# Linear attention into a routed mixture of experts: all row tiles of attention turned by VectorE, the first one-hot lanes by ScalarE, gates and routing half a pair of steps sooner

## The chip, the cores and the metric

The kernel runs on one core of a Trainium2 chip. The metric is the device time of one execution in microseconds; lower is better. TensorE (PE in the profile; PEld is its weight load) multiplies, VectorE (DVE) and ScalarE (ACT) work on tiles, GpSimd (POOL) multiplies by powers and issues the indirect transfers, SyncE (SP) issues nearly all other transfers. Each engine works through its own instructions in program order and waits at the head of its queue.

## The reference

Four sequences of 768 tokens, 8 heads of 64. Attention in blocks of 64: `intra = (q k^T * Dmask) v`, `inter = (q * lam^(pos+1)) kv_state`, then `kv_state = lam^64 * kv_state + (k * rev_pow)^T v`. The output, a row x of 512 numbers for each token, goes into a layer of 8 experts:

```python
logits = x @ w_gate                       # 8 numbers for each token
local_gate = sigmoid(x @ w_local)
e = argmax(logits) if s == 0 or local_gate < 0.5 else prev_e   # along the sequence
p = softmax(logits)
out[b, s] = p[e] * (relu(x[b, s] @ w1[e]) @ w2[e])
```

A token thus either takes its own best expert or that of its predecessor, and each row goes through one expert only.

## The kernel before

**Attention.** The tokens lie in 24 row tiles of 128 (`ORDER`: six chunks c of each of the four sequences b, so tile s is chunk s // 4 of sequence s % 4). A step s has five parts on TensorE: `scores` (into one of two pairs of PSUM banks, `sides`), `from_state` (queries times the state `kvs[b]`, into banks `po0`, `po1` for even s and `pl`, `pr` for odd s), `mix` (masked scores times values into the same banks; ScalarE copies the result to `xc[:, :, b]`), and `update` (keys times values, into the banks that held scores; VectorE adds the result to the state). VectorE's `masked` turns scores into `sm`, GpSimd's `prepare` makes the keys and queries with powers. From step 6 on two steps form a pair: the loop `for s in range(PAIRS, NS, 2)` issues the scores of s + 1 and s + 2, both `masked`, `from_state` of s and s + 1, what `middles[s]` lists, `mix` of both, what `betweens[s]` lists, `turn(s)`, `update` of both, the loads, what `lasts[s]` lists, `turn(s + 1)`. The order is written out by hand in a manual schedule for all five engines, so what stands earlier in this list is ahead in the engine's queue. Step s + 3's scores go into the same pair of banks as those of step s + 2 (s even).

**Rows.** `xc` holds x with features on partitions. The rows themselves go to `x_dram`, from which tiles of tokens of one expert are gathered later. There are two ways: `turned_rows` has VectorE transpose 32 x 32 blocks of a tile into a group of four tiles (`TURNED` says at which step), and `group_out` writes the group in four transfers whose pieces are 512 bytes; `rows_of` has TensorE turn the tile in four matmuls, ScalarE copy it, and SyncE write it in pieces of 2 KB. Tiles 0 to 13 and 20 to 22 take the first way, 14 to 19 and 23 the second. Each loop step sends up to two waiting group transfers; the rest follow the loop, ahead of the weights of the second tile of experts.

**Routing.** `gates(k)` multiplies chunk k by the gate weights (ScalarE copies the product), `logits(k)` turns it back, VectorE reduces it into `lt`. Routing is done in three `PARTS` (tiles 0 to 7, 8 to 11, 12 to 23): `fresh_experts` marks each token's own expert, `along_sequences` carries the expert along the sequence (a test against zero, `stay`, and a scan), `experts_of` makes `hot`, `ranks` numbers the tokens of each expert (`place`), `masks` makes one-hot lanes from the place, `first_tiles` and `first_ends` choose the experts of the first KA = 3 tiles, `tokens_to_first_tiles`, `brought` and `by_slots` turn this into indices `gidx`, with which `ahead` gathers the first tiles from the rows of the first 12 tiles of attention.

**Experts.** After the loop come three full tiles (`hidden`, `output`, with the rest of the routing between) and then eight units, one for each expert, of sums and products of halves. The weights are 2 MB each (`w1t`, `w2t`, two buffers of each), loaded by SyncE.

Of the kernel before, what the change touches and what calls it, by code (L numbers as in the profile page):

```python
# [42 lines left out]
TURNED = {**{r: r + 1 if r < PAIRS else r // 2 * 2 + 2 for r in range(3 * B)}, 12: 15, 13: 16, 20: 22, 21: 22, 22: 23}  # L43
# [26 lines left out]
def kernel(  # L70
# [96 lines left out]
    kvs = []  # L167
    for b in range(B):
        kvs.append(pows.tile([P, A, DH], F32, name=f"kv{b}"))
# [74 lines left out]
    def from_state(s):  # L244
        b, c = ORDER[s]
        head = heads[s] = place_of(s)
        if c:
            kv, qd = kvs[b], qds.pop(s)
            for a in range(A):
                for u in range(2):  # L250
                    rows = slice(DH * u, DH * u + DH)
                    nc.tensor.matmul(head(a, u), lhsT=kv[rows, a], rhs=qd[rows, a],  # L252
                                     start=(a < 2), stop=False, skip_group_check=True)
# [16 lines left out]
    def update(s):  # L270
        b, c = ORDER[s]
        x = inp.pop(s)
        if c + 1 < NC:
            kv, vn = kvs[b], x[:, 2].rearrange("p (a u d) -> p a u d", u=2, d=DH)
# [14 lines left out]
    def rows_of(s, px=None):  # L289
        if px is None:  # L290
            px = pg.tile([P, DM], F32, name="pk1")
        for a in range(A):
            nc.tensor.transpose(px[:, P * a:P * a + P], xc[:, a, ORDER[s][0]], ident)
        if s + 1 < NS:
            xn = att.tile([P, DM], F32, name="xn", bufs=4)
        else:
            xn = xlast
        nc.scalar.copy(xn.rearrange("p (j d c) -> p j d c", j=4, c=QP), px.rearrange("p (d j c) -> p j d c", j=4, c=QP))


        nc.sync.dma_start(out=x_dram[P * s:P * s + P, :], in_=xn)

    groups = {}

    def turned_rows(s):

        k = s // B
        if k not in groups:
            if k + 1 == NC:
# [50 lines left out]
    def constants_1():  # L360
# [8 lines left out]
        nc.gpsimd.memset(onesb, 1.0)  # L369
        nc.gpsimd.memset(ones8, 1.0)  # L370
# [35 lines left out]
    place = route.tile([P, 2, NT], I32, name="place")  # L406
    late = route.tile([P, NA], F32, name="late")
    taken = route.tile([P, E], F32, name="taken")
# [32 lines left out]
    def along_sequences(i, pr=pr):  # L441
# [8 lines left out]
        nc.vector.tensor_scalar(stay, prow, 0.0, None, ALU.is_equal)  # L450
# [7 lines left out]
    def experts_of(i):  # L458
# [9 lines left out]
    def ranks(i, pr=pr):  # L468
# [23 lines left out]
        nc.vector.tensor_scalar(place[:, 0, lo:hi], rank, P - 1, None, ALU.bitwise_and)  # L492
        nc.vector.tensor_scalar(place[:, 1, lo:hi], rank, -P, None, ALU.bitwise_and)

    def masks(i):

        lo, hi = PARTS[i]
        lane = onehots[i] = (act if i == 2 else route).tile([P, hi - lo, P], BF16, name=f"lane{i}", bufs=1)
        nc.vector.tensor_tensor(lane, countb.unsqueeze(1).broadcast_to([P, hi - lo, P]),
# [47 lines left out]
    def first_tiles():  # L547

        tiles = multiples(0, NA, counts[1], ALU.is_ge, 1)
        table = nows["table"] = rt.tile([P, 2, E], F32, name="table0", bufs=1)  # L550
# [7 lines left out]
    def first_ends():  # L558

        table, ends, more, tiles = (nows[n] for n in ("table", "ends", "over", "tiles"))  # L560
# [7 lines left out]
        nc.vector.tensor_tensor(table[:, 0], ends, taken, ALU.subtract)  # L568
        nc.vector.tensor_copy(table[:, 1], taken)

    def tokens_to_first_tiles():
# [5 lines left out]
        nc.vector.scalar_tensor_tensor(to, late, float(P * AWAY), to, ALU.mult, ALU.add)  # L577
        owners(0, 0, KA, nows["ends"], 0)
# [966 lines left out]
```

## Time and profile before

| | |
|---|---|
| median of 3 runs | 403.49 us (403.45 to 404.9) |
| the profiled execution | 403.04 us, span 401.3 us, mean granted clock 0.997 |
| busy, share of the span | PE 97%, PEld 90%, DVE 74%, ACT 54%, POOL 46% |
| DMA | 90.67 MB, mean 226 GB/s |

The span reaches from the first to the last instruction. Attention fills the first 90 us; the first hidden layer of an expert starts at 90.91 us, the units at 137.62 us. A matmul's end in the profile is modelled, since matmuls overlap in the array; the distance between the starts of two groups is the better measure of what a group costs. An engine's idle time is given with the instruction that ended it.

### The profile page before, as it was taken

How to read it: one execution, taken by the hardware profiler on the slowest of the kernel's cores; microseconds unless marked ns; L12 is line 12 of the kernel's file. 1: busy time of each engine (PE TensorE's matmuls, PEld its weight loads, DVE VectorE, ACT ScalarE, POOL GpSimd, SP SyncE). 2: the span in 40 equal slices, each digit the busy share in tenths (PEclk: the TensorE clock that was granted, in tenths of full speed). 3: DMA queues.
4: the chain of work that ended last, by engine and by line, in shares of the span. 5: the costliest groups of instructions: out<-in, count | busy, mean ns of one | idle time of the engine just before them, and what ended most of it. 6: DMA issues, size and time to landing. Idle time of an engine off the chain costs nothing. (4 is left out here: it accounts for less than half of the span.)

```text
span 401.3 us, 9727 instructions
## 1 busy us (share of the span) xinstructions
PE 391.1 (97%) x3729; PEld 362.8 (90%) x3729; DVE 297.7 (74%) x570; ACT 215.4 (54%) x658; POOL 184.4 (46%) x228
## 2 busy tenths in 40 slices
PE   7999999999999999999999999999999999999994
PEld 6788988878679699999999999999999999999983
DVE  6876989947845889878868768686776868677931
ACT  4236355446715758767557755944854684460310
POOL 5589677330125312174272277157227605701741
PEclk9999999999999999999999999999999999999998
DMA  7999999999999977357346266273545606100101
GB/s 272 417 425 402 416 399 389 340 311 284 390 399 372 406 274 263 96 185 279 118 171 222 70 233 223 97 235 94 206 119 200 265 29 237 51 0 8 45 35 60
DMA packets 37145, 90.67 MB, mean 226 GB/s; under 512 B 3344, under 2 KB 12064, under 8 KB 35424
## 3 DMA queue, kind: packets, MB, share of 16 engines
q1 hardware_dynamic: 31920, 76.57, 52.1%
q0 software_dynamic: 5152, 13.38, 9.5%
q8 instruction: 31, 0.51, 0.5%
q14 instruction: 26, 0.21, 0.2%
q10 hardware_dynamic: 16, 0.00, 0.0%
HBM read 81.55 MB, written 12.91 MB: 235 GB/s over the span
## 5 line engine op out<-in xcount | busy, mean ns | idle before, releaser
L1207 POOL DMA_INDIRECT out_dram<-yq,sidxq x80 | 89.2, 1115 | 103.3 <-DVE yq L1195 69.9
L1152 PE MATMUL ps<-arena,s 128*128 128x148 f32 (+7 forms) x384 | 63.1, 307 | 0.0
L1152 PEld LDWEIGHTS ps<-arena,s 128*128 128x128 f32 x384 | 57.3, 190 | 0.4 <-DVE part L1336 0.3
L807 POOL DMA_INDIRECT xg<-x_dram,gidx x27 | 30.1, 1117 | 52.5 <-DVE w L1123 14.6
L1152 PE MATMUL po<-arena,w 128*128 128x148 f32 (+7 forms) x256 | 41.9, 307 | 0.0
L1152 PE MATMUL ps<-arena,w 128*128 128x148 f32 (+7 forms) x256 | 41.9, 307 | 0.0
L828 ACT COPY arena<-xlast 32x128 f32<-32x128 f32 x128 | 37.8, 295 | 4.8 <-DVE xlast L821 2.1
L1152 PEld LDWEIGHTS ps<-arena,w 128*128 128x128 f32 x256 | 38.3, 190 | 0.5 <-issue 0.5
L1152 PEld LDWEIGHTS po<-arena,w 128*128 128x128 f32 x256 | 38.2, 190 | 0.0
L188 POOL TENSOR_TENSOR qd<-inp,lamq 128x256 f32<-128x256 f32 x40 | 29.5, 759 | 16.7 <-DMA inp<-in_qkv_dram 6.5
L828 ACT COPY arena<-lg 32x128 f32<-32x128 f32 x120 | 35.5, 296 | 2.6
L1190 PE MATMUL pk<-h,w 128*128 128x148 f32 (+6 forms) x224 | 35.1, 310 | 0.0
L1190 PE MATMUL pk<-hsum,s 128*128 128x148 f32 (+6 forms) x224 | 35.1, 310 | 0.0
L1190 PEld LDWEIGHTS pk<-h,w 128*128 128x128 f32 x224 | 33.4, 190 | 0.0
L1190 PEld LDWEIGHTS pk<-hsum,s 128*128 128x128 f32 x224 | 33.4, 190 | 0.0
L256 ACT ACTIVATE kv<-kv,lamq 128x64 f32<-128x64 f32 x64 | 16.4, 335 | 24.0 <-PE po L252 24.0
L1171 ACT COPY arena<-xlast 32x128 f32<-32x128 f32 x88 | 26.9, 305 | 1.9
L194 POOL TENSOR_TENSOR kd<-inp,rev 128x256 f32<-128x256 f32 x40 | 23.8, 615 | 7.9 <-DMA inp<-in_qkv_dram 7.8
L1308 ACT ACTIVATE h<-ps 128x296 f32<-128x296 f32 (+6 forms) x14 | 6.4, 458 | 36.8 <-PE ps L1152 36.8
L225 DVE TENSOR_TENSOR sm<-ps,mask 128x512 f32<-128x512 f32 x30 | 19.2, 682 | 9.1 <-PE ps L217 9.0
L838 PEld LDWEIGHTS ps<-xt,w 128*128 128x128 f32 x192 | 22.1, 192 | 1.9 <-issue 1.0
L838 PE MATMUL ps<-xt,w 128*128 128x128 f32 x192 | 22.7, 276 | 0.0
(333 smaller groups left out, 777.1 us busy)
## 6 DMA issues: line engine op xcount, KB each, us to landing
w<-in_w_dram SPq DMA_DIRECT2D x22, 2048.0 KB, 9.4
inp<-in_qkv_dram SPq DMA_DIRECT2D x13, 1024.0 KB, 11.9
inp<-in_qkv_dram SPq DMA_DIRECT2D x14, 512.0 KB, 9.6
w<-in_w_dram SPq DMA_DIRECT2D x4, 1024.0 KB, 10.2
x_dram<-w SPq DMA_DIRECT2D x12, 256.0 KB, 9.6
inp<-in_qkv_dram SPq DMA_DIRECT2D x4, 768.0 KB, 10.8
x_dram<-xn SPq DMA_DIRECT2D x6, 256.0 KB, 8.4
out_dram<-yq,sidxq POOLq DMA_INDIRECT x80, 3.9
```

What stands on the lines that cost most here:

```text
L188: nc.gpsimd.tensor_tensor(qd[:, heads], x[:, 0].rearrange("p (a i) -> p a i", i=P)[:, heads], lamq[:, heads], ALU.mult)
L194: nc.gpsimd.tensor_tensor(kd.rearrange("p (h d) -> p h d", d=DH)[:, heads], x[:, 3].rearrange("p (h d) -> p h d", d=DH)[:, heads], rev[:, ...
L225: nc.vector.tensor_tensor(sm[:, u], ps[u], mask[:, u], ALU.mult)
L256: nc.scalar.mul(kv[:, a], kv[:, a], lamq[:, a, P - 1:P])
L807: nc.gpsimd.indirect_dma_start(out=xg, out_offset=None, in_=x_dram[:n, :], in_offset=bass.IndirectOffsetOnAxis(ap=gidx[i][:, j:j + 1], axi ...
L828: copy((xt(k) if callable(xt) else xt)[QP * j:QP * j + QP, :, at(k):at(k) + QP], blocks[QP * k:QP * k + QP, :, j])
L838: nc.tensor.matmul(ph[:, j], lhsT=w1t[w][:, d, P * f:P * f + P], rhs=xtt[i][:, d], start=(d == 0), stop=(d == DT - 1))
L1152: nc.tensor.matmul(to[:, j], lhsT=a[:, k, P * m:P * m + P], rhs=b[:, k], start=(new and not j and not k), stop=(k == 1), skip_group_check= ...
L1171: nc.scalar.copy(xu[QP * j:QP * j + QP, u % 2::2 - u % 2, :, P + QP // 2 * k:P + QP // 2 * k + QP // 2], blocks[QP * k:QP * k + QP, :, j]. ...
L1190: nc.tensor.matmul(to[:, m], lhsT=a[:, f, P * m:P * m + P], rhs=b[:, f], start=(new and not m and not f), stop=(f == FT // 2 - 1), skip_gr ...
L1207: last = nc.gpsimd.indirect_dma_start(out=out.rearrange("n (j d) -> (n j) d", j=4), out_offset=bass.IndirectOffsetOnAxis(ap=sidxq[:, u, i, ...
L1308: relus(hu[f, i][:, lo:hi, :W], c, ACT.Relu)
```

## The change

Every row tile takes the first way: `TURNED` now has all 24, and `rows_of` is gone. Tiles 16 and 17 are turned in the middle of step 20 (19.5 in the table), 18 and 19 after it, 20 and 21 in step 22, 22 and 23 after it. The groups of tiles 16 to 19 and 20 to 23 lie in buffers of the loads.

`masks` of the first two parts goes from VectorE (one comparison of the whole part) to ScalarE: one absolute value of (count - place) for each row tile of 128 x 128, then one ReLU of 1 minus that. `stay` of `along_sequences` goes from VectorE to ScalarE too.

The entries of `middles`, `betweens` and `lasts` move: `gates`, `along_sequences` and `ranks` stand at the end of a pair, where they were in the middle of the next, and `logits`, `fresh_experts` and `experts_of` in the middle of a pair, where they were at the end of the one before. `first_ends` goes to the middle of step 18, and choosing the owners of the first tiles goes out of `tokens_to_first_tiles` into `first_owners`, after `by_slots`. `LATE` puts masking of step 20 (in step 18) and of step 22 (in step 20) behind the middles. Two constants are made at step 2.

The state of all sequences lies in one tile, and the fading that follows `from_state` takes two sequences in a call: four calls for a pair instead of eight, after both `from_state`. `place` is made by one operation instead of two, `first_ends` has six instead of nine.

```diff
-TURNED = {..., 12: 15, 13: 16, 20: 22, 21: 22, 22: 23}
+TURNED = {..., 12: 14, 13: 15, 14: 16, 15: 17, 16: 19.5, 17: 19.5, 18: 20, 19: 20,
+          20: 22, 21: 22, 22: 23, 23: 23}
+LATE = [(20, 18), (22, 20)]
...
-            if c + 1 < NC:
-                for a in range(A):
-                    nc.scalar.mul(kv[:, a], kv[:, a], lamq[:, a, P - 1:P])
+    def fade(s, n=1):
+        b, c = ORDER[s]
+        if c and c + 1 < NC:
+            for a in range(A):
+                kv = kvs[:, b:b + n, a]
+                nc.scalar.mul(kv, kv, lamq[:, a, P - 1:P])
...
-            if k + 1 == NC:
+            if k > 3:
                 xn = load.tile([P, 4, DM], F32, name="inp").rearrange("p n m -> p (n m)")
...
-        nc.vector.tensor_scalar(stay, prow, 0.0, None, ALU.is_equal)
+        nc.scalar.activation(stay, prow, ACT.Relu, bias=1.0, scale=-1.0)
...
-        nc.vector.tensor_scalar(place[:, 0, lo:hi], rank, P - 1, None, ALU.bitwise_and)
-        nc.vector.tensor_scalar(place[:, 1, lo:hi], rank, -P, None, ALU.bitwise_and)
+        nc.vector.tensor_tensor(place[:, :, lo:hi], rank.unsqueeze(1).broadcast_to([P, 2, n]),
+                                bits.unsqueeze(2).broadcast_to([P, 2, n]), ALU.bitwise_and)
...
+        if i < 2:
+            back = rt.tile([P, hi - lo], F32, name=f"back{i}", bufs=1)
+            nc.scalar.mul(back, place[:, 0, lo:hi], -1.0)
+            for t in range(hi - lo):
+                nc.scalar.activation(lane[:, t], countb, ACT.Abs, bias=back[:, t:t + 1])
+            nc.scalar.activation(lane, lane, ACT.Relu, bias=1.0, scale=-1.0)
+            return
...
-        nc.vector.tensor_tensor(tiles, tiles, ends, ALU.add)
-        nc.vector.tensor_scalar(ends, ends, float(KA), None, ALU.min)
-        nc.vector.tensor_scalar(tiles, tiles, float(KA), None, ALU.min)
-        nc.vector.tensor_tensor(taken, tiles, ends, ALU.subtract)
+        nc.vector.tensor_scalar(ends, ends, -1.0, float(KA), ALU.mult, ALU.add)
+        nc.vector.scalar_tensor_tensor(taken, ends, 0.0, tiles, ALU.max, ALU.min)
...
+    def first_owners():
         owners(0, 0, KA, nows["ends"], 0)
...
     middles = {
-        8: gates(1, x[0]), 10: along_sequences(0, x[1]), 12: (ranks(0, x[1]), gates(2, x[0])),
-        14: along_sequences(1, x[1]), 16: (turn(16), ranks(1, x[1]), gates(3, x[0])),
-        18: logits(3, x[0]), 20: (by_slots(0, (0, 1), x[0]), gates(4, x[1]), rows_of(18, x[0])), 22: logits(4, x[0]),
+        8: (logits(1, x[0]), fresh_experts(0)), 10: experts_of(0, x[1]),
+        12: (logits(2, x[0]), fresh_experts(1)), 14: experts_of(1, x[1]),
+        16: logits(3, x[0]), 18: first_ends(),
+        20: (by_slots(0, (0, 1), x[0]), first_owners(), turn(19.5)), 22: logits(4, x[0]),
     betweens = {
-        8: constants_2, 10: constants_3, 14: masks(0), 16: first_tiles, 18: (masks(1), tokens_to_first_tiles()),
+        12: masks(0), 16: first_tiles, 18: (masks(1), tokens_to_first_tiles()),
         20: (prepare(NS - 1), ahead(0, 0), ahead(1, 1)),
     lasts = {
-        8: (logits(1), fresh_experts(0)), 10: experts_of(0), 12: (logits(2), fresh_experts(1)),
-        14: experts_of(1), 16: (rows_of(14, pl), rows_of(15, pr), first_ends()),
-        18: (rows_of(16, pl), rows_of(17, pr), brought(0, (0, 1))), 20: rows_of(19, x[1]),
+        6: gates(1, pl), 8: along_sequences(0, pr), 10: (gates(2, pl), ranks(0, pr)),
+        12: along_sequences(1, pr), 14: (gates(3, pl), ranks(1, pr)),
+        18: (gates(4, pl), brought(0, (0, 1))),
         22: (first_turned(x[1]), gates(NC - 1), rows_out(0)),
...
-                if r < NS:
+                if r < NS and (r, s) not in LATE:
                     masked(r)
...
+            fade(s, 2)
             if s in middles:
                 middles[s](free)
+            if (s + 2, s) in LATE:
+                masked(s + 2)
...
-            if s != 16:
-                turn(s)
+            turn(s)
...
             logits(NC - 1)
-            rows_of(NS - 1)
             moved(xtt[1], xq, (1,))
```

In the three tables of the diff the word `lambda x:` ahead of each entry is left out.

More of the change, by code (lines that the diff above doesn't have):

```diff
@@ L166 @@
     NS = len(ORDER)
-    kvs = []
-    for b in range(B):
-        kvs.append(pows.tile([P, A, DH], F32, name=f"kv{b}"))
+    kvs = pows.tile([P, B, A, DH], F32, name="kv")
     xc = att.tile([P, A, B, P], F32, name="xc", bufs=1)
@@ L287, in update @@
                 nc.vector.tensor_copy(kv, pk)
[L289 to L301, printed above, removed]
     groups = {}
@@ L456, in along_sequences, with experts_of @@
         nc.vector.tensor_tensor_scan(run, stay, prow, before, ALU.mult, ALU.add)
-    def experts_of(i):
+    def experts_of(i, pr=pr):
         lo, hi = PARTS[i]
@@ L549, in first_tiles @@
         tiles = multiples(0, NA, counts[1], ALU.is_ge, 1)
-        table = nows["table"] = rt.tile([P, 2, E], F32, name="table0", bufs=1)
+        nows["table"] = table0
         ends = nows["ends"] = rt.tile([P, E], F32, name="ends0", bufs=1)
@@ L887 @@
     middles = {
-        8: lambda x: gates(1, x[0]), 10: lambda x: along_sequences(0, x[1]), 12: lambda x: (ranks(0, x[1]), gates(2, x[0])),
-        14: lambda x: along_sequences(1, x[1]), 16: lambda x: (turn(16), ranks(1, x[1]), gates(3, x[0])),
-        18: lambda x: logits(3, x[0]), 20: lambda x: (by_slots(0, (0, 1), x[0]), gates(4, x[1]), rows_of(18, x[0])), 22: lambda x: logits(4, x[0]),
+        8: lambda x: (logits(1, x[0]), fresh_experts(0)), 10: lambda x: experts_of(0, x[1]),
+        12: lambda x: (logits(2, x[0]), fresh_experts(1)), 14: lambda x: experts_of(1, x[1]),
+        16: lambda x: logits(3, x[0]), 18: lambda x: first_ends(),
+        20: lambda x: (by_slots(0, (0, 1), x[0]), first_owners(), turn(19.5)), 22: lambda x: logits(4, x[0]),
     }
     betweens = {
-        8: constants_2, 10: constants_3, 14: lambda: masks(0), 16: first_tiles, 18: lambda: (masks(1), tokens_to_first_tiles()),
+        12: lambda: masks(0), 16: first_tiles, 18: lambda: (masks(1), tokens_to_first_tiles()),
         20: lambda: (prepare(NS - 1), ahead(0, 0), ahead(1, 1)),
@@ L896 @@
     lasts = {
-        8: lambda x: (logits(1), fresh_experts(0)), 10: lambda x: experts_of(0), 12: lambda x: (logits(2), fresh_experts(1)),
-        14: lambda x: experts_of(1), 16: lambda x: (rows_of(14, pl), rows_of(15, pr), first_ends()),
-        18: lambda x: (rows_of(16, pl), rows_of(17, pr), brought(0, (0, 1))), 20: lambda x: rows_of(19, x[1]),
+        6: lambda x: gates(1, pl), 8: lambda x: along_sequences(0, pr), 10: lambda x: (gates(2, pl), ranks(0, pr)),
+        12: lambda x: along_sequences(1, pr), 14: lambda x: (gates(3, pl), ranks(1, pr)),
+        18: lambda x: (gates(4, pl), brought(0, (0, 1))),
         22: lambda x: (first_turned(x[1]), gates(NC - 1), rows_out(0)),
@@ L949 @@
             from_state(s)
+            fade(s)
             if s == 5:
```

20 lines of the change are left out of this document (13 added, 7 removed).

## The prediction, made blind

> **What bounds the kernel now.** I read the page first: engines, DMA tenths, chain of waits. Its chain covers only the last microsecond, so the bound has to come from the engines.
>
> ```profile
> PE 391.1 (97%) x3729; PEld 362.8 (90%) x3729; DVE 297.7 (74%) x570; ACT 215.4 (54%) x658; POOL 184.4 (46%) x228
> ...
> DMA  7999999999999977357346266273545606100101
> ```
>
> TensorE is busy for 97% of the span, and it works in program order: time is won only by taking work out of its queue, or lost by making its head wait. The second row says that DMA is full for the first 14 slices of 10 us, so its arrivals stand close behind. Next the table by stretches, cut at the steps 16 to 19 of attention, the pair 20, one stretch that carries only rows of x to DRAM, and one of weights.
>
> ```profile
> 61.32:77.14 15.82, 15.43 (x303) 13.27 (x302) 14.79 (x43) 8.62 (x30) 9.35 (x14) 1.00 1.04 378
> 77.14:85.08 7.94, 7.61 (x158) 5.75 (x157) 4.21 (x15) 3.28 (x8) 3.64 (x4) 1.00 0.96 309
> ...
> 94.00:96.00 2.00, 2.00 (x20) 2.00 (x20) 1.76 (x12) 1.19 (x4) 0.00 (x0) 1.00 0.92 252
> 98.00:106.00 8.00, 8.00 (x45) 4.53 (x45) 6.46 (x32) 7.66 (x27) 0.00 (x0) 1.00 1.02 383
> ```
>
> Columns: length, busy time of PE, weight load, DVE, ACT, POOL, then clock (full throughout), DMA share and GB/s. Steps 16 to 19 have DVE busy for 14.79 of 15.82 us: VectorE is as full as TensorE there. Step 20 has half of DVE free. TensorE's own list of waits shows two in this region, both for VectorE's masked scores:
>
> ```profile
> PE ps L336 <- DVE sm L225: 0.4, 1, 0.4
> ...
> PE ps L447 <- DVE sm L225: 0.3, 1, 0.3
> ```
>
> **The change, part by part. A, TensorE loses seven turns of a row tile.**
>
> ```profile
> 68.31 0.66 PE L293 MATMUL pl<-ident,xc 128*128 128x128 f32 x4
> ...
> 69.33 1.16 PE L217 MATMUL ps<-inp 64*128 64x128 f32 x16
> ```
>
> (Timeline of TensorE: start, length, line.) Two tiles take 69.33 - 68.31 = 1.02 us, 0.51 each. Six (14 to 19) stood before the first hidden layer: -3.06 us. That is certain in size; whether it shows is the question. Tile 23 comes later (E).
>
> What the other engines take instead:
>
> ```profile
> L314 DVE STREAM_TRANSPOSE w<-xc 128x512 f32<-128x512 f32 x14 | 9.5, 692 | 0.0
> ...
> L499 DVE TENSOR_TENSOR lane<-countb,place 128x1024 bf16<-128x1024 bf16 (+2 forms) x3 | 3.7, 1246 | 0.0
> ...
> L844 ACT ACTIVATE h<-ps 128x512 f32<-128x512 f32 x6 | 3.6, 597 | 9.8 <-PE ps L838 9.7
> ...
> L1206 ACT ACTIVATE yq<-yq,gateq 128x128 f32<-128x128 f32 x10 | 3.1, 391 | 0.0
> ...
> L376 ACT ACT_TABLE_LOAD x1 | 1.3, 1283 | 1.4 <-PEq L1537 1.4
> ```
>
> (Groups: busy us, mean ns of one.) VectorE gains seven transposes of 0.69 us (4.8 us) and loses two lane masks (1.25 us, and some 0.7 for the one of half the columns). ScalarE loses seven row copies and gets the lanes. An absolute value with a per-partition bias over 128x128 is not in this trace; the nearest row is L1206, 128x128 with a per-partition factor: 10 in 3.1 us, 0.31 apart. Bounds: 0.20 (half of one's 391 ns) to 0.39 (no overlap). The closing ReLU over 1024 columns is at most two of L844, 1.2 us, and by its slope about 1.0. So lanes of part 0: 0.2 + 8 x 0.30 + 1.0 = 3.6 us (2.6 to 4.6).
>
> **B, a new wait in step 14.** The lanes of part 0 are issued in step 12, and behind them on ScalarE, in program order, stand `stay` and `carry` of `along_sequences(1)`; VectorE's scan waits for these; the scan reads bank `pr`, which `from_state(15)` on TensorE writes. All of it was free before, since `stay` and the lanes were VectorE's and the lanes came after the scan.
>
> ```profile
> 53.07 1.10 PE L282 MATMUL pk<-inp,kd 128*64 128x64 f32 x32
> ...
> 53.39 0.38 ACT L268 COPY xc<-pr 128x256 f32<-128x256 f32 x1
> ...
> 54.69 1.16 PE L217 MATMUL ps<-inp 64*128 64x128 f32 x16
> ...
> 56.82 0.43 PEld L252 LDWEIGHTS po<-qd,kv 64*64 64x64 f32 x16
> ...
> 58.10 1.28 DVE L225 TENSOR_TENSOR sm<-pk,mask 128x512 f32<-128x512 f32 x2
> ...
> 58.38 1.09 PE L265 MATMUL po<-sm,inp 128*64 128x128 f32 x16
> ...
> 59.30 0.27 DVE L450 TENSOR_SCALAR stay<-ps 4x128 bf16<-4x128 f32 x1
> ...
> 59.67 0.47 DVE L456 TENSOR_TENSOR_SCAN run<-stay,carry,ps 4x128 bf16<-4x128 bf16 x1
> ...
> 60.18 1.10 PE L282 MATMUL ps<-inp,kd 128*64 128x64 f32 x32
> ```
>
> On the old clock: ScalarE is done with step 13's copies at 53.77; + 3.6 lanes + 0.3 `stay` + 0.15 `carry` + 0.47 scan + 0.1 = 58.4. TensorE from 53.07, where mix(13) has ended: update 1.03 of its 1.10, `along_sequences` 0.15, two steps' scores 2.13 (54.69 to 56.82), `from_state(14)` 0.5 = 56.9. Wait 1.5 us. Then `experts_of(1)` writes the bank of step 15's scores, so it waits for masking that follows the scan: 1.28 less 0.5 of `from_state(15)`, 0.75. Less the 0.3 of L447 that goes: **+1.9** (0.9 to 2.9 with the bounds of the lanes).
>
> **C, steps 16 and 18.**
>
> ```profile
> 67.92 0.67 DVE L532 TENSOR_TENSOR more<-incl,whole 128x96 f32<-128x96 f32 x1
> ...
> 69.76 0.74 DVE L285 TENSOR_TENSOR kv<-pk,kv 128x256 f32<-128x256 f32 x2
> ```
>
> `first_tiles` takes VectorE 69.76 - 67.92 = 1.84 us and stands ahead of the two state additions. From the moment that masking frees the bank for `logits(3)`, VectorE has 0.6 + 1.28 masking, 0.3 reduction, 1.84, transpose 14 at 0.65, additions 0.74 = 5.4; TensorE has logits 0.6, a pair's mix 1.8 (58.38 to 60.18), update 1.03, scores(19) 1.0 = 4.4 before scores(20), whose bank the addition frees. The row turns that filled this place (1.02) are gone: it waits about 0.9 us, less the 0.4 of L336: **+0.5** (0 to 0.9).
>
> **D, steps 20 and 22.** Masking of step 22 now follows the reading of slots, `first_owners` and the transposes of 16 and 17.
>
> ```profile
> 77.94 1.12 PE L217 MATMUL ps<-inp 64*64 64x128 f32 x28
> ...
> 79.97 0.46 PE L683 MATMUL pk<-val,lane 128*128 128x6 bf16 x12
> ...
> 80.96 0.16 DVE L692 COPY got<-pk 128x6 f32<-128x6 f32 x1
> ...
> 85.08 0.90 PE L217 MATMUL ps<-inp 64*64 64x128 f32 x32
> ...
> 86.04 1.29 DVE L225 TENSOR_TENSOR sm<-ps,mask 128x512 f32<-128x512 f32 x2 [4.52 <-PE ps L217]
> ```
>
> VectorE sat idle 4.52 us here. Now: three steps like that at 80.96, 0.55 with their gaps, for the slots and three for the owners, 1.3 and 1.28 = 3.65 us after the slots' matmuls. TensorE has only mix(20) and mix(21), 1.8 us, before scores(23), which share a bank with scores(22): **+1.85** (1.2 to 2.2). The 28 matmuls at 77.94 took 0.2 more than the 32 at 85.08, a small wait of old: -0.2.
>
> **E, tile 23.** TensorE saves 0.5, but VectorE has two transposes where one stood, ahead of the marks of part 2.
>
> ```profile
> 96.80 0.17 DVE L439 SCALAR_TENSOR_TENSOR each<-lt,each 128x12 bf16<-128x12 f32 x1
> ...
> 97.34 0.33 PE L447 MATMUL pr<-identb,each 128*4 128x128 bf16 x3
> ```
>
> Marks are ready at 96.97, used at 97.34: slack 0.37. With +0.65 on VectorE, the use comes 0.25 later, not earlier: **+0.25** (-0.5 to +0.4). `stay` of part 2 on ScalarE stands where ScalarE lost a row copy: nothing.
>
> **At nothing:** fading the state with four wider calls for a pair starts one step later, ends at about the same time, and `kv` is next added after the update; the earlier constants, the shorter `first_ends` and merged `place` run beside TensorE. If that cover is gone each costs below 0.5. Gates and routing are moved, not added: same matmuls, same copies.
>
> **DMA.** Rows 14 to 19 and 23 went out in 2 KB pieces as they came; now in 512 B pieces and four tiles together, rows 20 to 23 at the very end, ahead of the weights of tile 1 in SyncE's queue.
>
> ```profile
> 91.58 2.90 SPq L321 DMA_DIRECT2D x_dram<-inp  x4
> ...
> 95.16 0.42 SPq L778 DMA_DIRECT2D w<-in_w_dram  x1
> ...
> 129.73 1.23 DVE L1123 TENSOR_TENSOR s<-w 128x1024 f32<-128x1024 f32 x1 [0.50 <-DMA w<-in_w_dram]
> ...
> 131.81 2.51 ACT L1171 COPY arena<-arena 32x128 f32<-32x128 f32 x8
> ...
> 136.83 0.97 DVE L1125 TENSOR_TENSOR arena<-arena 128x296 f32<-128x296 f32 x2 [1.15 <-ACT arena L828]
> ...
> 138.62 1.17 PE L1152 MATMUL ps<-arena,s 128*128 128x148 f32 x8
> ```
>
> From 95.16 the weights are one full stream; its landing for unit 0 releases VectorE at 129.73, then a transpose (to 131.6), ScalarE's copies from 131.81, VectorE at 136.83 to 137.79, TensorE at 138.62. Slack of TensorE against that landing: 0.83 at the end plus 0.2 before the copies, 1.0 us. This caps any gain. Price of the pieces: 94 to 96 us, 512 B only, moves 252 GB/s at share 0.92, so 274 full; weights 383/1.02 = 375. A 256 KB tile costs 0.96 instead of 0.70: +1.8 us for seven, at least 0 if 2 KB writes are as slow. The stream starts later by 1.2 (TensorE) + 0.65 (one more transpose) + 0.96 (a fourth tile), less 0.7 for the last row tile's own write: about 2.1 us, 1.1 beyond the slack, which is no more than TensorE's own delay below, so it adds nothing.
>
> The Trainium skill, "DMA: Bandwidth & Descriptors", section Specifications, puts the least piece for full rate at 512 B; by that the seven tiles cost no DMA time and the cap would loosen by up to 1.8 us, with the same sum. The trace disagrees, 274 against 375 GB/s, and the trace decides.
>
> **Sum:** -3.06 + 1.9 + 0.5 + 1.85 - 0.2 + 0.25 = +1.2 us on the profiled execution's 403.04 (span 401.3 and 1.7 around it), 404.2; the median of the three runs stands 0.45 above that execution, so **404.7**. Its own bounds: -0.9 to +3.0.
>
> **Rivals.** *The saving shows.* ScalarE's lanes run 0.2 apart, waits B and D shrink into softer overlaps, and TensorE arrives 2 to 3 us sooner. For it: VectorE's 4.52 us idle is room. Against: the order of the queues. Then the landing at 129.7 decides: gain 1.0, **402.5**. *The row writes decide, slower.* Place: SyncE's queue after step 22. If two writes of rows 16 to 19 are still unfinished (2 x 0.96) when rows 20 to 23 come, the stream shifts by 2.1 + 1.9 = 4.0, minus slack 1.0: +3.0, **406.5**. It decides from a shift of 2.2 on. For it: 1 MB more is held back to the end; against: step 20 leaves DMA at share 0.96, some of it idle. *The absolute value needs another table.* One load is in the trace, at the start; two more of its 1.28 us in front of `stay` add 2.6 to B: **407.3**. The Trainium skill, "ScalarE: Activation LUTs", section Table sets, counts abs and relu as fillers of every set; by that no load comes, and the one load for ReLU, Exp and copies agrees.
>
> **Chances.** Forecast (403 to 405.5) 0.55; saving shows 0.20; row writes 0.18; table 0.03; gain beyond the cap 0.04. Range 402.0 to 406.8. Within 0.5% is 401.5 to 405.5, about what a measurement can tell from no change: 0.70; faster 0.06 (gain beyond the cap, an edge of the second); slower 0.24 (row writes, table, an edge of the forecast).
>
> **What would show it.** Right: no L293; VectorE idle about 2 us before the scan of part 1, released by ScalarE; TensorE waits at `from_state` of 15, scores(20), scores(23), the last near 2 us; the first hidden layer at 91.5 to 92.5 instead of 90.9. Wrong: that layer before 90, ACT lanes below 2.6 us, or a second table load. The DMA rival is right if VectorE's first sum of unit 0 (L1123's successor) starts after 132 us and TensorE then waits.

## The result, and the profile after

The changed kernel takes 407.97 us (median of 4 runs, 407.21 to 409.82) where the kernel before takes 403.51: a ratio of 1.0109, 95% interval 1.0067 to 1.015. It is slower, by more than the forecast's range allowed. The profiled execution took 407.21 us with a span of 405.4, so 4.1 us of span are to be found between the two profiles.

The page of the changed kernel, engines and DMA slices:

```profile
PE 389.4 (96%) x3701; PEld 360.2 (89%) x3701; DVE 299.5 (74%) x566; ACT 213.4 (53%) x642; POOL 182.8 (45%) x230
...
DMA  7999999969999985177266175363536616100101
```

TensorE has 28 matmuls fewer, seven turns of four. But DMA, full from 10 to 140 us before, now has a hole in its ninth slice (81 to 91 us). TensorE's own waits of 10 to 160 us (us in total, times, longest) show two groups of new ones:

```profile
PE ps L217 <- DVE sm L225: 2.6, 3, 1.5
PE ps L1158 <- DVE arena L1131: 1.2, 1, 1.2
PE pr L441 <- DVE each L433: 0.7, 1, 0.7
...
PE ps L457 <- DVE sm L225: 0.5, 1, 0.5
PE ps L1158 <- DVE part L1333: 0.5, 1, 0.5
PE ps L217 <- DVE kv L289: 0.4, 1, 0.4
```

L217, L441 and L457 stand in attention and the routing; both L1158 are unit 0's products. Timelines of the changed kernel at the end of attention (TensorE, then SyncE):

```profile
85.81 0.43 PE L217 MATMUL ps<-inp 64*64 64x128 f32 x2 [1.54 <-DVE sm L225]
...
92.27 1.94 PE L838 MATMUL ps<-xt,w 128*128 128x128 f32 x15
...
93.58 4.71 SPq L311 DMA_DIRECT2D x_dram<-inp  x4
99.12 0.41 SPq L778 DMA_DIRECT2D w<-in_w_dram  x1
```

The first hidden layer starts 1.36 us later than before (90.91). The four last row writes start 2.0 us later than before (91.58) and take 4.71 us to issue instead of 2.90, so the weights of tile 1, behind them in SyncE's program, are issued 3.96 us later (95.16 before). At unit 0 (VectorE's chain, then TensorE), changed kernel:

```profile
133.61 1.22 DVE L1129 TENSOR_TENSOR s<-w 128x1024 f32<-128x1024 f32 x1 [2.74 <-DMA w<-in_w_dram]
...
139.26 1.17 PE L1158 MATMUL ps<-arena,w 128*128 128x148 f32 x8
141.62 1.25 PE L1158 MATMUL ps<-arena,s 128*128 128x148 f32 x8 [1.19 <-DVE arena L1131]
...
144.39 1.27 PE L1158 MATMUL ps<-arena,s 128*128 128x148 f32 x8 [0.52 <-DVE part L1333]
```

and the fourth group of products in the kernel before, with the sum that releases it:

```profile
140.23 0.42 DVE L1327 TENSOR_TENSOR part<-part,ps 128x296 f32<-128x296 f32 x1
...
140.71 1.27 PE L1152 MATMUL ps<-arena,s 128*128 128x148 f32 x8
```

The landing for unit 0 is 3.88 us late. TensorE comes to unit 0 1.64 us late (139.26 against 137.62), is 3.00 late at the second group (141.62 against 138.62) and 3.68 at the fourth (144.39 against 140.71). That is nearly the whole loss. Before, the sum for the fourth group ended at 140.65 and TensorE used it at 140.71: there was next to no slack. The profile of the kernel before has one peculiarity: a stop of TensorE of some 0.8 us near 84 us, which the profiles of its variants with more row writes and with earlier weights, below, lack (first hidden layer at 90.12 and 90.10). Against the former (unit 0 at 136.83) TensorE is 2.4 us late, and not 1.64.

### The profile page after: what moved, and what is told of

Same layout as the page of the kernel before. It is cut to its first block, busy times and chain, and to the rows that moved or that the text cites. A ratio compares the mean times of both kernels' runs of the same rounds, so it can differ in the third digit from the quotient of the medians.

```text
span 405.4 us, 9594 instructions
## 1 busy us (share of the span) xinstructions
PE 389.4 (96%) x3701; PEld 360.2 (89%) x3701; DVE 299.5 (74%) x566; ACT 213.4 (53%) x642; POOL 182.8 (45%) x230
## 5 line engine op out<-in xcount | busy, mean ns | idle before, releaser
L1158 PE MATMUL ps<-arena,s 128*128 128x148 f32 (+7 forms) x384 | 63.3, 308 | 1.8 <-DVE arena L1131 1.2
L1158 PEld LDWEIGHTS ps<-arena,s 128*128 128x128 f32 x384 | 57.2, 190 | 2.6 <-issue 1.4
L1158 PE MATMUL po<-arena,w 128*128 128x148 f32 (+7 forms) x256 | 41.9, 307 | 0.0
L1158 PE MATMUL ps<-arena,w 128*128 128x148 f32 (+7 forms) x256 | 41.9, 307 | 0.0
L1158 PEld LDWEIGHTS ps<-arena,w 128*128 128x128 f32 x256 | 38.2, 190 | 0.5 <-issue 0.5
L1158 PEld LDWEIGHTS po<-arena,w 128*128 128x128 f32 x256 | 38.2, 190 | 0.0
L188 POOL TENSOR_TENSOR qd<-inp,lamq 128x256 f32<-128x256 f32 x40 | 28.4, 732 | 19.7 <-PE po L252 17.4
L260 ACT ACTIVATE kv<-kv,lamq 128x128 f32<-128x128 f32 (+1 forms) x36 | 11.1, 379 | 20.6 <-PE pr L252 13.1
```

Of the source, the lines that this page charges most:

```text
L188: nc.gpsimd.tensor_tensor(qd[:, heads], x[:, 0].rearrange("p (a i) -> p a i", i=P)[:, heads], lamq[:, heads], ALU.mult)
L260: nc.scalar.mul(kv, kv, lamq[:, a, P - 1:P])
L1158: nc.tensor.matmul(to[:, j], lhsT=a[:, k, P * m:P * m + P], rhs=b[:, k], start=(new and not j and not k), stop=(k == 1), skip_group_check= ...
```

## The experiments

Each is compared with the kernel before, run beside it. The sets ran on several chips: the kernel before took 403.5 to 403.7 us in the first and third set, 438.4 in the second, 419.4 and 420.3 in the last two, where a later part (behind unit 0) is slower. So ratios to before are read, and of the profiles of the slower chips only what lies ahead of unit 1.

**The rows alone, and the cost of late weights.** First, the kernel before with the new way of rows and nothing else; second, the kernel before with four more row writes ahead of the weights.

```diff
-TURNED = {..., 12: 15, 13: 16, 20: 22, ...}           # before_rows; rows_of(...) goes
+TURNED = {..., 12: 14, ..., 16: 19.5, ..., 23: 23}
...
         for k, j in turned_out:                        # before_more
             group_out(k, j)
+        for j in range(4):                             # rows 20 to 22 once more, into x_more
+            nc.sync.dma_start(out=x_more[...], in_=groups[NC - 1][QP * j:QP * j + QP, :3]...)
```

> The kernel before with the way of the rows alone changed: tiles 14 to 19 and 23 turned by VectorE at the steps of the changed kernel and written as groups, everything else as before. TensorE loses six turns, 3.06 us, and gets none of the new waits of steps 14 and 22, so it reaches the first hidden layer at 88 to 88.5 us instead of 90.9. Queue theory: the row writes are still held back (1 MB more behind the last load, some 3.5 us) and take all of it: unit 0's landing stays at 129.5 to 130.5 us, 402.8 to 403.8 us in all. Waits theory: the saving shows, 400.4 to 401.

> The kernel before with four more writes of 192 KB in 512-byte pieces (rows 20 to 22 once more, to a place of their own) ahead of the weights of tile 1: the cost of held-back row writes by itself, TensorE's work unchanged. At 252 GB/s they are 3.1 us; about 1.1 us of a delay of the stream was given back on the way to unit 0 in the changed kernel, so the landing comes 2.0 us later, near 131.7. With no slack behind the landing (the fourth group of unit 0's products started 0.06 us after its sum was ready): 405.0 us. With the 1.0 us of slack of the prediction: 404.0. If transfers are hidden behind TensorE: 403.0.

Measured: rows alone 404.61 us, ratio 1.003 (1.0007 to 1.0052); more writes 406.08, ratio 1.0064 (1.0039 to 1.0089), 2.43 us over before's 403.65. Rows alone, TensorE's waits and unit 0:

```profile
PE ps L337 <- DVE sm L226: 1.6, 1, 1.6
PE ps L218 <- DVE kv L286: 0.9, 1, 0.9
...
130.78 1.23 DVE L1123 TENSOR_TENSOR s<-w 128x1024 f32<-128x1024 f32 x1 [2.12 <-DMA w<-in_w_dram]
...
138.80 1.25 PE L1152 MATMUL ps<-arena,s 128*128 128x148 f32 x8 [0.59 <-DVE arena L1125]
141.57 1.27 PE L1152 MATMUL ps<-arena,s 128*128 128x148 f32 x8 [0.52 <-DVE part L1327]
```

More writes, SyncE and VectorE:

```profile
93.01 3.50 SPq L1013 DMA_DIRECT2D x_more<-inp  x4
97.55 0.42 SPq L779 DMA_DIRECT2D w<-in_w_dram  x1
...
132.16 1.23 DVE L1127 TENSOR_TENSOR s<-w 128x1024 f32<-128x1024 f32 x1 [3.73 <-DMA w<-in_w_dram]
```

With rows alone the landing is 1.05 us late (130.78 against 129.73); the second group of products is 0.18 late, the fourth 0.86. So the slack is 0.87 at the one and 0.19 at the other, and the kernel pays by the latter: about 1 us. With more writes the weights are issued 2.39 us later, land 2.43 later, and the time is 2.43 us longer, more than either price expected. That the two numbers are equal is in part chance: the landing less the slack of 0.19 comes to 2.24, and in the profile TensorE's wait of 2.19 us ahead of the second group (140.19) is followed by half the granted clock, with which the next two groups take 2.10 and 1.64 us instead of some 1.0, so that the fourth starts 3.22 us late (143.93). The saving of TensorE did not come at all: VectorE, with the transposes, makes TensorE wait 1.6 and 0.9 us, and the first hidden layer starts at 90.05, as in the profile of the kernel with more writes (90.12), whose TensorE has all its turns.

**The rest of the change alone**: the changed kernel with tiles 14 to 19 and 23 turned by TensorE again.

```diff
-        20: (by_slots(0, (0, 1), x[0]), first_owners(), turn(19.5)), ...
+        20: (by_slots(0, (0, 1), x[0]), first_owners(), rows_of(18, x[0])), ...
+        16: (rows_of(14, pl), rows_of(15, pr)),        # and 16, 17, 19, 23 where they stood
```

> The changed kernel with the way of the rows as before (tiles 14 to 19 and 23 turned by TensorE and written one by one in pieces of 2 KB): the rest of the change alone. TensorE has its 3.06 us of turns again, and VectorE 4.8 us less to do. If the two parts add up (rows alone came to +1.0 us, the change to +4.3): +3.0 to +3.5 us over before, with TensorE 2.5 to 3.5 us late at the first hidden layer and the landing of unit 0 late by as much. If what costs is VectorE having both the transposes and the moved routing at once: waits at steps 16 to 22 go with the transposes, and it is within 1.5 us of before.

Measured 405.69 us, ratio 1.0052 (1.0035 to 1.0069), +2.2 us. In its profile (span 404.3) the landing is 3.24 us late (132.97), and TensorE comes to unit 0 2.89 late by itself (140.51): either alone would cost nearly as much. 1.18 us of it is a wait for ScalarE's copy of a row tile at 80.37, which neither whole kernel has, so the split isn't a clean one. With +1.0 for the rows, the parts come to 3.2; the change itself, run again in this set, to 5.8:

> The changed kernel itself, unedited, beside the other three on one chip, as their measure: 1.0 to 1.3% over the kernel before, landing of unit 0's first weights 3.5 to 4.2 us later than before.

Measured 409.3 us (6 runs), ratio 1.0143 (1.0111 to 1.0175). So the parts do not quite add up: together they cost 2.6 us more than one by one in this set, and 1.3 with the 4.5 us of the first. The windows of this run (PE, PEld, DVE, ACT, POOL busy, clock, DMA share, GB/s), and below them one of the first profile of the change:

```profile
86.00:88.00 2.00, 1.49 (x34) 1.25 (x38) 2.00 (x4) 0.44 (x2) 0.69 (x1) 0.79 0.73 174
88.00:90.00 2.00, 2.00 (x40) 1.67 (x32) 1.38 (x3) 0.00 (x0) 0.00 (x0) 0.50 0.63 189
90.00:92.00 2.00, 2.00 (x28) 1.83 (x28) 1.06 (x3) 0.25 (x1) 0.00 (x0) 0.85 0.61 106
```

```profile
88.00:90.00 2.00, 1.98 (x33) 1.64 (x28) 1.85 (x5) 0.30 (x2) 0.00 (x0) 1.00 0.79 171
```

Right behind the wait of 1.54 us at scores(23) TensorE is granted half its clock for some 3.4 us: 2 x (0.21 + 0.50 + 0.15) = 1.7 us lost. The first profile has the same wait without it.

**Weights sent earlier.** The first layer's weights of tile 1 go to the head of step 22, all of them in the changed kernel, half of them there, and all of them in the kernel before.

```diff
+            if s == NS - 2:
+                weights_of(0, 1, 1, (1,))              # early_half: only w1t[1][:, :DT // 2]
...
         for k, j in turned_out:
             group_out(k, j)
-        weights_of(0, 1, 1, (1,))
```

> The changed kernel with one transfer moved: the first layer's weights of tile 1 (2 MB) are issued at the head of step 22, ahead of the row writes of tiles 16 to 23, into the stretch around 84 to 90 us in which DMA moves 181 GB/s. Queue theory (the row writes held back to the end shift the stream of weights, unit 0's landing sets the loss): the landing for unit 0 falls from 133.6 to about 130.5 us, TensorE's waits of 1.2 and 0.5 us at unit 0 go, and TensorE's own lateness of 1.65 us is left: 404.7 to 405.2 us against 407.2 in the profile of the change. Waits theory (TensorE's new waits in steps 14 and 22 and what follows from them set the loss, the transfers only follow): the time stays at 407 to 408.

> The changed kernel with only half of the first layer's weights of tile 1 (1 MB instead of 2) moved to the head of step 22, so that less lies ahead of the last load and of the gather of tile 2. Queue theory: 1 MB, 2.8 us at 375 GB/s, goes into the stretch in which DMA moves 181 GB/s, the landing of unit 0 falls to 131 us or below, and the time by 2 to 2.8 us against the change. VectorE theory: under 1 us.

> The kernel before with the same transfer moved, as a control. Queue theory: TensorE waits for no weights in it, so nothing changes, 403.0 to 403.7 us. If the earlier transfer were a gain by itself and not the cure of the lateness, it would be near 400 to 401.

Measured: all 406.76 us (1.0074, 1.0051 to 1.0097); half 407.14 (1.0076, 1.0048 to 1.0103), 2.2 below the change in its set; in the kernel before 405.61 (1.0044, 1.0027 to 1.0061). Half of the weights helps the change clear of the noise; for all of them the intervals overlap (1.0109 is from another set). In both profiles TensorE no longer waits at unit 0, and both have the half clock behind scores(23), so early_half can be read beside the change of its own set, whose TensorE comes to unit 0 at the same time (141.33 and 141.32). The fourth group of products, early_half and then the change:

```profile
144.41 1.27 PE L1161 MATMUL ps<-arena,s 128*128 128x148 f32 x8
```

```profile
146.13 1.27 PE L1158 MATMUL ps<-arena,s 128*128 128x148 f32 x8 [0.52 <-DVE part L1333]
```

The waits for the late weights are thus worth 1.72 us, of the 2.2 between the medians. The profile with half the weights has a span of 404.7, 3.4 over before: 1.7 of clock and some 1.7 of TensorE's lateness. The control failed its forecast: earlier weights cost the kernel before 2 us. In its profile (SyncE, then TensorE):

```profile
90.76 6.51 SPq L321 DMA_DIRECT2D x_dram<-inp  x4
100.65 0.09 SPq L1014 DMA_DIRECT2D w<-in_w_dram  x1
...
100.81 2.02 PE L848 MATMUL pk<-w,h 128*128 128x512 f32 x2 [1.77 <-ACT xt L828]
```

With 2 MB ahead of them the row writes take 6.51 us to issue instead of 2.90. Behind them stands a conditional reload of the second layer's weights, which is not taken (0.09 us), but the first output of tile 0, which reads them, starts only 0.16 us after SyncE has passed it at 100.65. TensorE waits 1.77 us, and half the clock follows. (The profile names a copy of ScalarE as the releaser; the same wait in no_late_swap, below, is put down to the DMA and ends 0.21 us after the reload has been passed.)

**Bytes or order.** Two kernels bring the row writes of tiles 16 to 19 forward, one of them on two chips: their bytes taken early from an older group (the rows 16 to 19 in DRAM then hold other tokens), or written in halves as soon as they are turned. A third exchanges neighbours in SyncE's program.

```diff
+            if s == NS - 4:                            # stale_rows
+                for j in range(4):
+                    group_out(4, j)                    # in_=groups[2 if k == 4 else k]...
...
+            if r // B == 4:                            # split: in turn(), after tiles 17 and 19
+                for j in range(4 if r % 2 else 0):
+                    group_out(4, j, r % B - 1, r % B + 1)
...
-        for k, j in turned_out:                        # swap
+        for k, j in turned_out[:-4]:
             group_out(k, j)
         weights_of(0, 1, 1, (1,))
+        for k, j in turned_out[-4:]:
+            group_out(k, j)
```

> The changed kernel, where the four writes of the group of tiles 16 to 19 are issued at the head of step 20 and take their bytes from the group of tiles 8 to 11, which lies ready: the rows 16 to 19 in DRAM then hold other tokens, so that part of the computation is left out; all transposes, bytes and pieces stay. It moves 1 MB from behind the last load into the stretch before 88 us, and no weights ahead of a gather. Queue theory: three writes of about 1.04 us go from in front of the weights, the landing of unit 0 falls from 133.6 to about 130.5 us, and TensorE's own lateness is left: 405.0 to 405.6 us. If TensorE's waits set the loss: 407.2 to 408.4, as the change.

> The kernel of stale_rows once more (rows 16 to 19 in DRAM filled early, at the head of step 20, from the buffer of tiles 8 to 11, so these rows hold other tokens), on a chip shared with the change itself. Queue theory: the landing of unit 0 falls by about 3 us against the change, TensorE waits under 0.5 us there, and the time falls by 2.0 to 2.8 us, which leaves TensorE's own lateness of 1.65 us. VectorE theory (VectorE is full in steps 16 to 23, and whatever is taken away there another wait takes its place): the landing falls as well, but the time falls by less than 1 us.

> The changed kernel, with the group of tiles 16 to 19 written in two halves, each issued as soon as its two tiles are turned (eight transfers of 128 KB instead of four of 256 KB). Queue theory: some 0.5 to 1 MB goes before 90 us that went behind, the landing of unit 0 falls by 1.5 to 2.5 us from 133.6, and so does the time: 405.5 to 406.5 us. If the writes' place does not matter: 407.2 to 408.4.

> The changed kernel with two neighbours in SyncE's program exchanged at the end of attention: the first layer's weights of tile 1 are issued ahead of the four writes of the last group of rows (tiles 20 to 23) instead of behind them. Nothing is sent into the empty stretch before 88 us, and the bytes ahead of unit 0's weights stay the same. Order theory (the weights start late because they stand in SyncE's program behind writes that wait for VectorE's last transposes, 93.58 us in the change, and take 4.7 us to issue): they are issued at 92.4 to 93.5 us instead of 99.1 to 100.0, the landing for unit 0 falls by 2 to 3 us, TensorE's waits there shrink below 0.5 us, and the kernel stands 0.5 to 0.8% over before instead of 1.1 to 1.4%. Backlog theory (the bytes held back are what shifts the stream): landing and ratio stay.

Measured: 1.0117 (1.0055 to 1.018) and, on the chip of the change's 1.0143, 1.0098 (1.0067 to 1.0128); split 1.0136 (1.007 to 1.0201); swap 1.0118 (1.0072 to 1.0165). The second stale_rows, SyncE, VectorE and windows:

```profile
95.61 3.57 SPq L311 DMA_DIRECT2D x_dram<-inp  x4
99.94 0.63 SPq L778 DMA_DIRECT2D w<-in_w_dram  x1
...
135.61 1.23 DVE L1132 TENSOR_TENSOR s<-w 128x1024 f32<-128x1024 f32 x1 [2.70 <-DMA w<-in_w_dram]
...
92.00:96.00 4.00, 4.00 (x43) 2.82 (x38) 3.00 (x7) 1.61 (x5) 1.00 (x1) 1.00 0.49 153
96.00:100.00 4.00, 4.00 (x39) 4.00 (x38) 3.27 (x19) 2.07 (x7) 0.00 (x0) 1.00 0.79 207
```

Here 1 MB less stands behind the last load, and the landing is where it was (135.61; 135.33 in the run of the change beside it). The time is 1.6 us below the change's, between what the two theories expected, and the intervals overlap. DMA is half idle from 92 to 96 us, because the next transfers in SyncE's program are row writes that wait for VectorE's last transposes, and the weights stand behind them: they are issued at 99.94, at 100.03 in the change beside it. So taking bytes out of the queue isn't enough. Nor is the order. The exchange stands at 1.0118 where the order theory expected 0.5 to 0.8% over before, which is what the backlog theory expected; and in no_late_swap, below, which has the exchange too, the weights are issued 5.9 us sooner than in no_late (93.36 and 99.28) and land only 0.4 us sooner (132.75 and 133.16). The two kernels' own windows, before and then changed:

```profile
80.00:88.00 8.00, 7.67 (x143) 5.82 (x142) 3.05 (x8) 3.12 (x7) 3.41 (x4) 1.00 0.99 319
88.00:92.00 4.00, 4.00 (x47) 2.82 (x43) 3.31 (x7) 1.88 (x5) 1.00 (x1) 1.00 0.86 283
80.00:110.00 30.00, 29.67 (x308) 22.21 (x306) 21.08 (x76) 18.54 (x54) 5.78 (x6) 1.00 0.97 326
```

```profile
80.00:88.00 8.00, 6.29 (x172) 5.40 (x172) 7.18 (x19) 1.24 (x4) 3.63 (x4) 1.00 0.66 206
88.00:92.00 4.00, 3.98 (x55) 2.73 (x48) 2.88 (x7) 1.29 (x4) 0.39 (x1) 1.00 0.78 190
80.00:110.00 30.00, 27.57 (x334) 20.70 (x335) 24.50 (x86) 15.51 (x49) 4.63 (x5) 1.00 0.90 290
...
110.00:120.00 10.00, 10.00 (x88) 8.22 (x88) 5.02 (x15) 2.24 (x5) 2.39 (x2) 1.00 1.04 401
```

The change sends 8 x 113 + 4 x 93 = 1276 KB less from 80 to 92 us, but what counts is what is still missing when both run at full rate. From 80 to 110 us it moves 290 GB/s where the kernel before moves 326: 30 x 36 = 1080 KB less, which at 401 GB/s is 2.7 of the 3.9 us by which the landing is late. The same window gives 289 GB/s in no_late_swap (2.8 us; landing 3.0 late), 259 in stale_rows_2 (5.0; 5.9), 264 in the change beside it (4.6; 5.6), and 316 with rows alone (0.7; 1.05), where 8 x 111 + 4 x 14 = 944 KB were missing at 92 us and most was made good by 110. So the landing goes, to within 1.2 us, by the idle time of DMA that is not made good ahead of the full stretch, whichever transfer SyncE's program holds back. This is a reading across kernels; no run changes the idle time alone.

**Waits of TensorE.** Masking of step 22 ahead of the reading of slots again, alone and with the two ways of earlier weights; both waits moved elsewhere; and waits of two lengths put into the kernel before.

```diff
-LATE = [(20, 18), (22, 20)]                            # no_late, no_late_half, no_late_swap
+LATE = [(20, 18)]
...
-        12: lambda: masks(0), ...                      # lanes_mask
+        14: lambda: masks(0), ...                      # and turn(19.5) behind masked(22)
...
         for u in range(2):                             # before_wait3, before_wait5
+            for _ in range(3 if s == NS - 1 and u else 0):
+                nc.vector.transpose(xlast, mask[:, 0]...)
             nc.vector.tensor_tensor(sm[:, u], ps[u], mask[:, u], ALU.mult)
```

> The changed kernel with one of its two deferrals taken back: masking of step 22 stands ahead of the reading of slots, the owners and two transposes in step 20 again, instead of behind them. The wait of 1.54 us at scores(23) goes, TensorE reaches the first hidden layer at 90.5 to 91.2 us. Length theory: the last transposes, row writes and the landing of unit 0 come 1.0 to 1.5 us sooner, 1.0 to 1.5 us less than the change (409.3 and 408.0 in its two sets, 404.9 over before's 403.5 plus 4.5). Clock theory: the stretch at half the clock at 87 to 91 us goes too, 2.2 to 3.2 us less than the change, 1.5 to 2.5 us over before.

> The same, and half of the first layer's weights of tile 1 issued at the head of step 22 as in early_half. Both theories: the landing of unit 0 falls to 131 us or below and TensorE waits less than 0.3 us there; what is left is TensorE's own lateness. Clock theory with the queue theory: within 1.0 us of before, 403.5 to 404.5 us where before is 403.5. If something else sets the time: 405.5 or more.

> The same exchange, and masking of step 22 taken back ahead of the reading of slots as in no_late, so that TensorE has no wait over 1 us. Order and clock theory together: 0.2 to 0.5% over before (TensorE's own lateness of 0.8 to 1.7 us is left), no stretch at half the clock behind 86 us. If something else sets the time: 0.8% or more over before.

> The changed kernel with the two costliest waits of TensorE undone: the lanes of part 0 one pair of steps later (behind the scan of part 1 instead of ahead of it), and the transposes of tiles 16 and 17 behind the masking of step 22 instead of ahead of it. TensorE reaches the first hidden layer 2.5 to 3.4 us sooner, at 88.9 to 89.8 us instead of 92.3. Waits theory: all of it shows, 404.6 to 405.5 us. Queue theory: the last transposes and row writes follow TensorE, but there is as much of them behind the last load, so the landing falls by only 1.5 to 2.5 us, and TensorE waits at unit 0 for the rest: 405.5 to 406.5.

> The kernel before with three more transposes of 128 x 512 on VectorE (0.66 us apart, into a tile that nothing reads yet) between the two halves of the masking of step 23, so that TensorE waits about 0.95 us at mix(23) and nothing else changes. A wait costs its length in both theories: 1.0 to 1.7 us over before (the upper end if VectorE is late at the marks of part 2 as well), and the clock stays at full rate behind it, as it did behind all eleven waits of 0.8 to 1.3 us seen before unit 1 so far.

> The same with five transposes: TensorE waits about 2.25 us at mix(23). Length theory (a wait of TensorE costs its length): 2.3 to 3.0 us over before. Clock theory (a wait of about 1.5 us or more is followed, in most executions, by some 3.4 us at half the clock, which costs 1.7 us more): 4.0 to 4.7 us over before, with a granted clock of 0.5 from about 90 to 93 us.

Measured: no_late 1.0096 (1.006 to 1.0132), with half the weights earlier 1.0047 (1.001 to 1.0084), with the exchange 1.0064 (1.0028 to 1.0099); lanes_mask 1.0161 (1.0098 to 1.0224); waits of 0.8 and 2.3 us 1.0047 (1.001 to 1.0084) and 1.0097 (1.0057 to 1.0137). So taking out the wait at scores(23) may help (the change's own 1.0109 and 1.0143 are from other chips, and the intervals overlap), but it is 4.0 us (2.5 to 5.5) over before where the clock theory expected 1.5 to 2.5. In its profile the wait and the half clock are gone, but TensorE comes to the first hidden layer at 92.22, in the change at 92.27; smaller waits took the place, one of 0.72 us at scores(22) for VectorE's additions (0.42 in the change), and the landing is only 0.45 us sooner (133.16). With half of the weights earlier about half a per cent is left, 2.0 us (0.4 to 3.5) where at most 1.0 was expected; in its one profile, of its longest execution (426.03 us), the waits at unit 0 are there again (1.05 and 0.52 us). lanes_mask did not help: its first hidden layer starts at 95.04, and not at 88.9 to 89.8. Its longest wait of TensorE in steps 14 to 22, and a window behind it:

```profile
PE pk L326 <- DVE sm L225: 1.4, 1, 1.4
...
70.00:74.00 4.00, 4.00 (x54) 3.67 (x54) 2.89 (x9) 1.26 (x4) 0.85 (x2) 0.65 0.95 347
```

With the lanes one pair later TensorE waits 1.43 us at the logits of step 16 instead, and gets the half clock there: here another order gave another wait. In no_late_swap (SyncE; TensorE's waits):

```profile
93.87 8.48 SPq L311 DMA_DIRECT2D x_dram<-inp  x4
102.71 0.09 SPq L1022 DMA_DIRECT2D w<-in_w_dram  x1
...
PE pk L848 <- DMA w<-in_w_dram: 1.6, 1, 1.6
```

The row writes, now behind 2 MB of weights, hold SyncE for 8.48 us, and the output of tile 0 waits for the reload behind them, as in the control above. The waits at unit 0 are gone, but because TensorE comes there 1.5 us later than in no_late (140.72 and 139.22); the weights land at nearly the same time.

Behind the wait of 2.29 us put into the kernel before the clock stays full in the profile; the first hidden layer starts at 92.90, 2.0 us later than before and 2.8 later than in the variants without the stop (90.1). So it does not bear out that such a wait always brings the half clock; its ratio (4.1 us, 2.4 to 5.7) fits both theories.

**Two tiles only**: the kernel before with tiles 16 and 17 turned by VectorE. The transposes stood behind mix(20) and mix(21), so the rows of 16 and 17 hold those of 20 and 21.

```diff
-TURNED = {**{r: ...
+TURNED = {16: 20, 17: 20, **{r: ...
```

> The kernel before with tiles 16 and 17 alone turned by VectorE, in step 20 where it stood idle for 4.52 us, and written in four transfers of 128 KB; all else as before. TensorE loses two turns, 1.02 us. Queue theory: 0.5 MB is held back to 86 us, and the stretch from 88 to 95 us, where DMA moves 284 to 311 GB/s, takes most of it, so TensorE's saving moves the end of attention, the last row writes and the landing together: 402.4 to 403.1 us. If any held-back row write is paid for in full behind the landing (0.5 MB, 2 us, less 1.0): 404.5.

Measured 437.31 us against 438.38, ratio 1.0003 (0.9966 to 1.0039): no gain that shows, though the interval (-1.5 to +1.7 us) does not exclude the forecast one of 0.4 to 1.1 us. No version here is shown to beat the kernel before.

## Why the prediction was wrong

**A**, seven turns off TensorE, was right in size (3729 to 3701 matmuls); behind the new waits nothing of it was left.

**B**: the lanes of part 0 on ScalarE, and the wait for what stands behind them, in the changed kernel:

```profile
55.04 0.22 ACT L495 ACTIVATE back<-place 128x8 f32<-128x8 int32 x1
55.30 2.45 ACT L497 ACTIVATE lane<-countb,back 128x128 bf16<-128x128 bf16 x8
57.77 1.06 ACT L498 ACTIVATE lane<-lane 128x1024 bf16<-128x1024 bf16 x1
...
59.10 0.47 DVE L450 TENSOR_TENSOR_SCAN run<-stay,carry,pr 4x128 bf16<-4x128 bf16 x1 [1.41 <-ACT carry L449]
```

3.8 us of lanes (forecast 3.6), 0.31 us from one absolute value to the next (0.30), VectorE's scan late as described. No second table load came. The starts of mix(12) and mix(16) on TensorE, before and then changed:

```profile
51.27 1.09 PE L265 MATMUL po<-sm,inp 128*64 128x128 f32 x16
...
65.48 1.09 PE L265 MATMUL po<-sm,inp 128*64 128x128 f32 x16
```

```profile
52.67 1.09 PE L269 MATMUL po<-sm,inp 128*64 128x128 f32 x16
...
68.78 0.98 PE L269 MATMUL po<-sm,inp 128*64 128x128 f32 x14
```

The lateness grows from 1.40 to 3.30 us: +1.9, the number forecast. The place was not: at `from_state(15)`, where 1.5 us were forecast, TensorE waits some 0.3 (59.33 to 59.62), since it comes there later than assumed. The rest is in smaller waits: for the marks of part 1 (0.33), for VectorE's additions to the state (0.21), at the bank of `experts_of(1)` (0.52) and at `logits(3)` (0.24). That the sum agrees is in part luck.

**C, D, E**: at scores(20), where C forecast 0.9, TensorE waits 0.1 (72.71); 0.42 came at scores(22) instead (79.89). D waits 1.54 us and some 0.46 more for the second bank, 2.0 where 1.85 was forecast; E adds 0.28 (1.64 at unit 0 less 1.36 at the first hidden layer) for 0.25. TensorE's sum was +1.24, and the profiles say +1.64, or 2.4 against a kernel before without its stop. So the sum is near by offsetting errors. (Added end to end, the bounds of its parts are -1.7 and +3.1, not -0.9 and +3.0; the outcome does not hang on it.) What was put at nothing was not quite nothing: of the 1.40 us at mix(12) about 0.6 is `logits(2)`, only moved ahead, and 0.8 has gathered in the steps up to there.

**DMA is the step that failed**: "the stream starts later by ... about 2.1 us, 1.1 beyond the slack, which is no more than TensorE's own delay below, so it adds nothing". Three terms of it were wrong. The start: VectorE's last transposes came 2.0 us late as said (1.2 + 0.65), but issuing the four writes took 1.8 us more, where 0.26 stood for the fourth tile; the issue is 3.96 us late. In the kernel before, the change, rows alone and more writes alike the landing follows this issue by 34.4 to 34.6 us. The use of DMA: that row writes held back leave DMA idle was only the rival's argument, and the 1080 KB missing by 110 us are not made good in the full stretch that follows. The slack: 1.0 was nearly right for the second group of products (0.87) and was read at that one place; two groups later there was 0.2, and that decides. With the slack of 0.2, a start 2.1 us late would have given 403.04 + 2.1 - 0.2 + 0.45 = 405.4; with the landing 3.9 late, 407.2.

**The rivals.** The row writes, slower, had the place (SyncE's queue after step 22), the sign and nearly the time (406.5), with 0.18; its sign for a test, VectorE's first sum of unit 0 after 132 us, came at 133.61. Its two late writes were there (issued at 91.30, just ahead of the four at 93.58), but its mechanism was not enough: taking them away left the landing where it was, since SyncE then waited for VectorE's last transposes. "The saving shows" had named the queue's order as what speaks against it, and no saving showed.

**The half clock** was in no term. In the set of the second run of the change it goes with longer times: the execution at a mean clock of 1.0 took 407.9 us, those at 0.996 and below 408.8 to 411.3. In the first set one at 0.999 took 408.43, so it doesn't explain alone why the medians (407.97, 409.3) lie above the profiled 407.21.

What stays open: why some long waits bring it and others do not; why the two parts cost more together; and about 1.7 us of the earlier weights' result (406.76, where about 405 was expected; its profiled execution of 406.66 would be 404.96 without its 1.7 us of half clock, but executions at nearly full clock are no faster).

## What to carry to other kernels

When DMA is full for a long stretch, follow each transfer's place in its issuer's program back to what it waits for: an idle stretch of DMA ahead of the full one is lost as far as it isn't made good before the full one begins, whatever is moved behind it, and a transfer that isn't even taken holds up whoever waits for its place. Read slack not at the next instruction behind a landing but at the next few of the chain; the smallest decides. A saving on a full engine, paid for on another that is full at the same steps, comes back as waits.

## What the runs showed of the hardware

Long waits of TensorE and the clock, over the 20 profiles, from 20 to 165 us: of 17 waits of 1.43 to 2.29 us, 7 were followed by some 3.4 us at a granted clock of 0.5, which cost 1.7 us each; of 12 waits of 0.79 to 1.29 us, none was. The longest without it was 2.29 us. The Trainium skill, "TensorE: Matmul & The Clock Gate", Part 1, says that the clock falls to half after about 3.4 us of idling, judged in windows of that length that run freely; the windows would fit a price that comes in some executions only, but here a wait of 1.43 us, less than half as long as that, was enough.

Row writes in pieces of 512 bytes took SyncE longer to issue where more stood ahead of them: four of 192 KB 2.9 us in the kernel before and 6.5 behind 2 MB of weights; four of 256 KB 3.6 us in stale_rows_2, 4.7 in the change, 8.5 behind 2 MB of weights.
